# Spectral layer and gated FFN on one core: the stretch before the FFN's first product is rebuilt around two row pairs

## The chip, the cores and the metric

One core of a Trainium2 chip. The metric is the device time of one execution in microseconds (us): 515.73 us before, the median of three runs (515.6 to 515.79). The engines are PE (matrix products), DVE (vector), ACT (activation), POOL (GpSimd) and SP, which here only issues transfers. PSUM is where PE writes its results; DVE and ACT read them from there.

## The reference, cut to what matters

```python
x = A_x                                   # 1 x 2048 x 576, bf16
X = rfft2(layernorm(x)) * (w_r + 1j*w_i)  # over rows and columns
h = x + irfft2(X)                         # bf16
a = layernorm(h)
out = h + (gelu(a @ w_gate) * (a @ w_up)) @ w_down     # 576 -> 4608 -> 576
```

The Fourier transforms are computed as matrix products with sine and cosine tables.

## The kernel before, in words

**Layout.** The 2048 rows of x are 16 tiles `h` of 128 rows by 576 columns, kept in `h_sb`. Two neighbouring tiles are a pair `g = h // 2` (0 to 7).

**Stages.** (1) Layer norm and forward transform, to about 60 us. (2) Inverse transform. `i3` (L541, L542) makes the two spectra `EO0` and `EO1`. `inv_cols(x, g)` (L567) multiplies one pair of one spectrum by column tables: six products of 128 x 290 into one PSUM tile `cs_ps`, which ACT scales into a bf16 tile `cs` (L576; for x=1, g=0 half is done by DVE, L578 and L579). `add_rows(g)` (L652) multiplies the `cs` tiles of a pair, x = 0 and 1, by row tables `G16`: sixteen products of 64 rows by 288 columns, into two PSUM tiles `y_ps`, one for each tile of the pair. `add_h` (L663, DVE) adds each to `h_sb`. (3) The FFN's layer norm of each tile: mean and variance by DVE (`stats2`: L118 to L120) or by two ACT passes whose sums POOL finishes (`stats_act`: L125, then L129 to L131); POOL takes the power -0.5 (L135, L136); DVE normalises the row with each block of 64 columns written twice (`norm2`, L677); a DMA transposes it into `hl` (`flip`, L689), four tiles to one `hl` of 512 columns. (4) The FFN in four chunks of four tiles. A chunk has 36 blocks: 18 products of 64 x 512 with gate and up weights into a PSUM tile `gu` (L758), gelu by ACT (L766), product by DVE into `P_sb` (L767). Then four times 72 products with `w_down` into `acc` (L778).

**What orders the work.** The order on each engine is written by hand: each engine runs its instructions in the order of the program and waits where one needs another. All PSUM tiles of stages 2 to 4 (`eo_ps`, `cs_ps`, `y_ps`, `gu`, `acc`) share four buffers, called "two"; a new tile waits until an older one has been read. `g_sb`, the gelu's output, has three buffers. SP issues in its own order: weight transfers (`load_wd`, `load_gu`) and the transposes of `flip`.

**Ahead of the first `gu` product**, which needs the transposed tiles 0 to 3, the kernel computes all 16 `inv_cols`, the `add_rows` of pairs 0 to 4, and the statistics, rows and transposes of tiles 0 to 3. The dictionary `todo` places the rest behind given blocks of the FFN: `add_rows` of pairs 5, 6, 7, and `stats2`, `norm2` and `flip` of tiles 4 to 15.

Of the kernel before, what the change touches and what calls it, by code (L numbers as in the profile page):

```python
# [9 lines left out]
ACT = mybir.ActivationFunctionType  # L10
# [10 lines left out]
P = 128  # L21
S = 2048
H = 16
# [17 lines left out]
def kernel_body(  # L41
# [24 lines left out]
    def two(name):  # L66
        return psum.tile([P, 2, 512], FP32, name=name, tag="two", bufs=3)
# [54 lines left out]
    def ln_act(h):  # L122
        for i, fn in ((0, ACT.Identity), (1, ACT.Square)):
            junk = roll.tile([P, D], BF16, name="junk", tag="junk", bufs=2)
            A.activation(junk[:], h_sb[:, h, :], fn, accum_out=sums[:, h, i : i + 1])  # L125
# [432 lines left out]
            )  # L558

    cs = {}  # L560

    def inv_cols(x, g):

        ps = two("cs_ps")
        for e in range(2):
            for jt in range(NJT):
                T.matmul(  # L567
                    ps[:, e, 0:JP],
                    lhsT=EO[x][:, e, jt, 2 * g : 2 * g + 2].rearrange("p h e k l -> p (h e k l)"),
                    rhs=DT[:, jt, :, e, :] if jt < 2 else DI[:, :, e, :],  # L570
                    start=(jt == 0),
                    stop=(jt == NJT - 1),
                )
        t = eop.tile([P, 2, JP], BF16, name="cs", tag="cs", bufs=H)
        if x == 0 or g:
            A.activation(t[:], ps[:, :, 0:JP], ACT.Copy, scale=Y_SCALE)  # L576
        else:
            A.activation(t[:, 0, :], ps[:, 0, 0:JP], ACT.Copy, scale=Y_SCALE)  # L578
            V.tensor_scalar(t[:, 1, :], ps[:, 1, 0:JP], Y_SCALE, None, op0=ALU.mult)  # L579
        cs[x, g] = t  # L580


    n = len(order)
    for i in range(n + 1):
        last = i >= n
        if not last:
            f2(order[i])
        if i == 0:
            twiddles()
        if 1 <= i <= n:  # L590
            f3(order[i - 1], 0)
        if i >= 3 and not last:
            i3(order[i - 3], 0)
        if 1 <= i <= n:
            f3(order[i - 1], 1)
            if i == 1:
                sums_of(order[0])
            else:
                wmul(order[i - 2], i - 1, order[i - 1])
        if i >= 3 and not last:  # L600
            i3(order[i - 3], 1)
        if not last:
            f2(order[i] + 8)
        if i == 0:
            weights()
        if i >= 3:
            for jt in range(0 if last else 2, NJT):
                i3(order[i - 3], jt)
        if last:
            wmul(order[i - 1], i)  # L610
        if i == 1:
            late_tables()
            scr_pool.__exit__(None, None, None)
            eop = ctx.enter_context(tc.tile_pool(name="eop", bufs=1, side="right"))
            EO = [eop.tile([P, 2, NJT, H, 2, 4, 8], BF16, name=f"EO{x}") for x in range(2)]
    for g in range(3):
        inv_cols(0, g)
    for jt in range(NJT):
        i3(order[6], jt)
    inv_cols(0, 3)  # L620
    inv_cols(0, 4)
    for jt in range(NJT):
        i3(order[7], jt)

    spw.__exit__(None, None, None)
    spec.__exit__(None, None, None)
    fp = ctx.enter_context(tc.tile_pool(name="ffn", bufs=1))
    P_sb = fp.tile([P, NFT, 4 * P], BF16, name="P_sb")
    wd_b = fp.tile([P, NFT - NWA, D], BF16, name="wd_b")

    def load_wd(f0):
        nc.sync.dma_start(wd_b[:, f0 : f0 + NWA, :], wd_view[:, NWA + f0 : 2 * NWA + f0, :])

    load_wd(0)


    ln2 = {}

    def add_rows(g):


        ys = [two("y_ps") for _ in range(2)]
        for b in range(2):
            for x in range(2):
                if b == 0:
                    cv = cs[x, g][:].rearrange("p t (q a) -> p t q a", q=2)[:, :, :, 0 : JH - 1]
                else:
                    cv = cs[x, g][:, :, 1:J].rearrange("p t (q a) -> p t q a", q=2)[:, :, :, ::-1]
                for t in range(2):
                    for i in range(2):  # L650
                        rows = slice(64 * i, 64 * i + 64)
                        T.matmul(  # L652
                            ys[i][:, b, 0:DH],
                            lhsT=G16[rows, b * t, x, :],
                            rhs=cv[rows, t],
                            start=(x == t == 0),
                            stop=(x == t == 1),
                        )
        return ys

    def add_h(h, ys):
        hv = h_sb[:, h, :].rearrange("p (b a q) -> p b q a", b=2, q=2)
        V.tensor_tensor(hv, hv, ys[h % 2][:, :, 0:DH].rearrange("p b (q a) -> p b q a", q=2), ALU.add)  # L663

    def add_both(g):
        ys = add_rows(g)
# [23 lines left out]
            hl[h // 4 % 2][:, :, q : q + P], ln2[h][:].rearrange("p r b k -> p (r b k)"), transpose=True  # L690
        )

    def stats_act(h):
        ln_act(h)
        ln_fin(mv2, h)
        ln_rstd(rstd2, mv2, h, h + 1)

    inv_cols(1, 0)
    inv_cols(1, 1)
    inv_cols(0, 5)  # L700
    ys = add_rows(0)
    add_h(0, ys)
    add_h(1, ys)
    stats2(0)
    inv_cols(1, 2)
    ys = add_rows(1)
    stats_act(1)
    inv_cols(0, 6)
    add_h(2, ys)
    norm2(0)  # L710
    flip(0)
    add_h(3, ys)
    inv_cols(0, 7)
    stats2(2)
    norm2(1)
    flip(1)
    inv_cols(1, 3)
    stats_act(3)
    inv_cols(1, 4)
    norm2(2)  # L720
    flip(2)
    inv_cols(1, 5)
    norm2(3)
    flip(3)
    load_wd(NWA)
    inv_cols(1, 6)
    add_both(2)
    inv_cols(1, 7)
    add_both(3)
    add_both(4)  # L730

    todo = {}
    for h in range(4, H):
        b = 6 * (h // 2 - 2)
        if h >= 10 and h % 2 == 0:
            todo.setdefault(b, []).append((add_both, h // 2))
        todo.setdefault(b, []).append((stats2, h))
        b = h // 4 * NFT - NFT + 3 * (h % 4) + 2 + 6 * (h < 8)
        todo.setdefault(b, []).append((norm2, h))
        todo.setdefault(b + 1, []).append((flip, h))  # L740

    blk = 0
    groups = pre
    NG = NFT // FQ
    for tcnk in range(4):
        for gi in range(NG):
            fa = gi * FQ
            w = groups.pop(0)
            n = tcnk * NG + gi + 2
            if 3 <= n < 4 * NG:  # L750
                groups.append(load_gu(n))
            for i in range(FQ):

                gu = two("gu")
                for r in range(NR):
                    for c in range(2):
                        rows = slice(64 * c, 64 * c + 64)
                        T.matmul(  # L758
                            gu[:, c, :],
                            lhsT=w[rows, r, i * P : (i + 1) * P],  # L760
                            rhs=hl[tcnk % 2][rows, r, :],
                            start=(r == 0),
                            stop=(r == NR - 1),
                        )
                g_sb = roll.tile([P, 4 * P], FP32, name="g_sb", tag="g_sb", bufs=3)
                A.activation(g_sb[:], gu[:, 0, :], ACT.Gelu_apprx_tanh)  # L766
                V.tensor_tensor(P_sb[:, fa + i, :], g_sb[:], gu[:, 1, :], ALU.mult)  # L767
                for fn, h in todo.pop(blk, ()):
                    fn(h)
                blk += 1  # L770
        for st in range(4):
            h = tcnk * 4 + st
            last = h == H - 1
            acc = two("acc")
            for c in range(2):
                cc = slice(c * DH, (c + 1) * DH)
                for f in range(NFT):
                    T.matmul(  # L778
                        acc[:, c, 0:DH],
                        lhsT=P_sb[:, f, st * P : (st + 1) * P],  # L780
                        rhs=wd_a[:, f, cc] if f < NWA else wd_b[:, f - NWA, cc],
                        start=(f == 0),
                        stop=(f == NFT - 1),
                    )
                if last:
                    V.tensor_tensor(h_sb[:, h, cc], h_sb[:, h, cc], acc[:, c, 0:DH], ALU.add)  # L786
                    nc.sync.dma_start(out_view[:, h, cc], h_sb[:, h, cc])
            if not last:
                hv = h_sb[:, h, :].rearrange("p (b n) -> p b n", b=2)
                V.tensor_tensor(hv, hv, acc[:, :, 0:DH], ALU.add)  # L790
                if tcnk == 3:
                    nc.sync.dma_start(out_view[:, h, :], h_sb[:, h, :])
        if tcnk < 3:
            nc.sync.dma_start(
                out_view[:, tcnk * 4 : (tcnk + 1) * 4, :],
                h_sb[:, tcnk * 4 : (tcnk + 1) * 4, :],
            )
# [46 lines left out]
```

## Time and profile before

| | |
|---|---|
| runs | 515.6, 515.73, 515.79 us |
| profiled execution | 515.73 us; its span (first to last instruction) 514.0 us, so 1.7 us lie around it |
| busy share of the span | PE 97%, DVE 40%, ACT 30%, POOL 7% |
| granted PE clock | 0.999 of full speed |
| end of stage 1, start of the first `cs_ps` product | 60.6 us |
| first `gu` product | 84.67 us |
| one `gu` block on PE | 1.95 us (342 products in 37.08 us on the chain) |
| `add_rows` of a pair behind an FFN block | 0.99 us of PE (x16) |

Times in the trace are counted from the start of the span. Of each instruction, the profile has start, duration, what it waited for before it, and what waited for it. The chain of work is followed back from the last instruction to what released it; it gives the length of the stretches that set the end. Instructions of one engine overlap a little: the next one's record often starts before the former's ends, so the distance between two starts (the pitch) is shorter than a record.

### The profile page before, as it was taken

To read this page: it belongs to the slowest core of one execution; us is meant where nothing else is said; L and a number is where in the kernel's file an instruction comes from. 1 tells how busy PE (TensorE), PEld (TensorE's weight loads), DVE (VectorE), ACT (ScalarE), POOL (GpSimd) and SP (SyncE) were. 2 spreads that over 40 slices of the span, in tenths; PEclk is the share of its full clock that TensorE was granted. 3 is DMA by queue.
4 is the path that set the end of the run, shared out by engine and by line. 5 is a ranking of instruction groups with operands and counts; after the bars stand their busy time and mean duration, and the time that the engine had idled before them with its cause. 6 is when DMAs were issued, how large, how long until landed. Compare 5 with 4: busy or idle time off the path is not lost.

```text
span 514.0 us, 9918 instructions
## 1 busy us (share of the span) xinstructions
PE 498.3 (97%) x4369; PEld 295.3 (57%) x4369; DVE 206.5 (40%) x381; ACT 153.5 (30%) x262; POOL 34.6 (7%) x94
## 2 busy tenths in 40 slices
PE   6989998999999999999999999999999999999996
PEld 2457765555557774444467754444577544444774
DVE  8979957566551003533321034333301233333000
ACT  8688974322221002233310013323200132323000
POOL 8700012111110000000000000000000000000000
PEclk9999999999999999999999999999999999999999
DMA  8964049799772009998740069988600477780000
GB/s 282 244 132 138 1 140 229 141 186 186 142 143 61 1 1 190 191 200 157 159 76 0 1 148 182 210 155 157 120 1 0 110 156 161 157 156 2 13 13 24
DMA packets 88459, 61.25 MB, mean 119 GB/s; under 512 B 24288, under 2 KB 87136, under 8 KB 88416
## 3 DMA queue, kind: packets, MB, share of 16 engines
q1 hardware_dynamic: 88128, 59.44, 56.8%
q0 software_dynamic: 288, 1.18, 0.8%
q8 instruction: 34, 0.56, 0.5%
q14 instruction: 9, 0.07, 0.1%
HBM read 52.65 MB, written 2.36 MB: 107 GB/s over the span
## 4 chain that ended last, share of the span: by engine, by line
PE 91%; DVE 5%; ACT 1%; POOL 1%; DMA 1%; issue 1%; POOLq 0%; DVEq 0%; ACTq 0%
PE gu L758 55%; PE acc L778 28%; PE f2t L259 2%; PE pq_ps L442 1%; PE cs_ps L567 1%; PE eo_ps L542 1%; PE eo_ps L541 1%; PE y_ps L652 1%; PE f2t L247 1%; DMA Bt<-hrow 1%; PE gh_ps L457 1%; PE gh_ps L458 1%; PE f L268 1%; DVE st L119 0%; DVE h_sb L663 0%
## 5 line engine op out<-in xcount | busy, mean ns | idle before, releaser
L758 PE MATMUL gu<-Bt,wgu 64*128 64x512 bf16 x2592 | 280.9, 376 | 0.7 <-DMA Bt<-hrow 0.7
L758 PEld LDWEIGHTS <-wgu 64*128 64x128 bf16 x2592 | 131.0, 94 | 148.6 <-issue 1.6
L766 ACT ACTIVATE g_sb<-gu 128x512 f32<-128x512 f32 x144 | 86.0, 597 | 305.9 <-PE gu L758 305.9
L767 DVE TENSOR_TENSOR P_sb<-g_sb,gu 128x512 bf16<-128x512 f32 x144 | 98.7, 685 | 162.1 <-ACT g_sb L766 162.1
L778 PEld LDWEIGHTS <-P_sb 128*128 128x128 bf16 x1152 | 112.4, 98 | 30.6 <-issue 2.4
L778 PE MATMUL acc<-wd_b,P_sb 128*128 128x288 bf16 x768 | 99.3, 286 | 0.0
L790 DVE TENSOR_TENSOR h_sb<-h_sb,acc 128x576 bf16<-128x576 bf16 x15 | 11.3, 754 | 119.2 <-PE acc L778 119.2
L778 PE MATMUL acc<-wd_a,P_sb 128*128 128x288 bf16 x384 | 52.3, 286 | 0.5 <-DVE h_sb L786 0.5
L247 PE MATMUL f2t<-h_sb,ident 128*128 128x512 bf16 x41 | 12.3, 422 | 4.5 <-DMA h_sb<-in_A_x_dram 4.5
L677 DVE TENSOR_SCALAR hrow<-h_sb,mv,rstd 128x1152 bf16<-128x1152 bf16 x16 | 13.8, 865 | 1.9 <-POOL rstd L136 1.9
L136 POOL TENSOR_TENSOR rstd<-rstd,mhalf 128x1 f32<-128x1 f32 (+2 forms) x21 | 14.0, 666 | 1.8
L567 PE MATMUL cs_ps<-DT,EO 128*128 128x290 bf16 x64 | 12.5, 286 | 0.6 <-DVE h_sb L663 0.4
L663 DVE TENSOR_TENSOR h_sb<-h_sb,y_ps 128x576 bf16<-128x576 bf16 x16 | 11.7, 784 | 2.1 <-PE y_ps L652 2.1
L135 POOL TENSOR_SCALAR rstd<-mv 128x1 f32<-128x1 f32 (+2 forms) x21 | 4.8, 230 | 113.4 <-DVE mv L120 112.6
L442 PE MATMUL pq_ps<-DT,Bt 128*128 128x290 bf16 x64 | 12.4, 287 | 0.0
L541 PE MATMUL eo_ps<-TI,Zt 128*128 128x256 bf16 x48 | 11.5, 272 | 0.4 <-DVE Zt L516 0.4
L542 PE MATMUL eo_ps<-TI,Zt 128*128 128x256 bf16 x48 | 11.5, 273 | 0.1
L567 PEld LDWEIGHTS <-EO 128*128 128x128 bf16 x96 | 8.9, 96 | 4.5 <-issue 1.3
L247 PEld LDWEIGHTS <-ident 128*128 128x128 bf16 x45 | 4.7, 104 | 11.4 <-issue 5.0
L259 PE MATMUL f2t<-F,xn 128*128 128x256 bf16 x64 | 9.7, 274 | 1.6 <-DVE xn L139 1.6
L125 ACT ACTIVATE junk<-h_sb 128x576 bf16<-128x576 bf16 x16 | 10.7, 670 | 1.4 <-DMA h_sb<-in_A_x_dram 0.9
L652 PE MATMUL y_ps<-cs,G 64*128 64x288 bf16 x128 | 9.8, 283 | 1.1 <-DVE h_sb L663 0.9
(113 smaller groups left out, 246.2 us busy)
## 6 DMA issues: line engine op xcount, KB each, us to landing
wgu<-in_B_w_gate_dram SPq DMA_DIRECT2D x48, 432.0 KB, 5.2
wgu<-in_B_w_up_dram SPq DMA_DIRECT2D x48, 432.0 KB, 6.6
wd_b<-in_B_w_down_dram SPq DMA_DIRECT2D x2, 1728.0 KB, 8.8
h_sb<-in_A_x_dram SPq DMA_DIRECT2D x3, 576.0 KB, 6.3
wd_a<-in_B_w_down_dram SPq DMA_DIRECT2D x1, 1728.0 KB, 9.1
out_dram<-h_sb SPq DMA_DIRECT2D x3, 576.0 KB, 3.4
WR<-in_A_w_r_dram SPq DMA_DIRECT2D x1, 650.2 KB, 9.1
WI<-in_A_w_i_dram SPq DMA_DIRECT2D x1, 650.2 KB, 11.5
```

What stands on the lines that cost most here:

```text
L136: G.tensor_tensor(dst[:, sl], dst[:, sl], mhalf[:, sl], ALU.pow)
L247: T.matmul(dst, lhsT=ident[:], rhs=h_sb[:, 2, 0:512], start=True, stop=True)
L259: T.matmul(f2t[:, h % 2, t * 2 * P : (t + 1) * 2 * P], lhsT=x[:, d0 : d0 + P], rhs=F16[:, n : n + 2, :], start=(n == 0), stop=(n == 1),)
L442: T.matmul(ps[:, par, 0:JP], lhsT=Bt[:, t, col], rhs=DT[:, t // 2, par] if t < 4 else DF[:, par], start=(t == par), stop=(t == 4),)
L541: T.matmul(ps[:, b], lhsT=zl(*z0), rhs=TI[:, kk_, 1:3, :], start=True, stop=False)
L542: T.matmul(ps[:, b], lhsT=zl(*z1), rhs=TI[:, kk_, 0:2, :], start=False, stop=True)
L567: T.matmul(ps[:, e, 0:JP], lhsT=EO[x][:, e, jt, 2 * g : 2 * g + 2].rearrange("p h e k l -> p (h e k l)"), rhs=DT[:, jt, :, e, :] if jt < 2 ...
L652: T.matmul(ys[i][:, b, 0:DH], lhsT=G16[rows, b * t, x, :], rhs=cv[rows, t], start=(x == t == 0), stop=(x == t == 1),)
L758: T.matmul(gu[:, c, :], lhsT=w[rows, r, i * P : (i + 1) * P], rhs=hl[tcnk % 2][rows, r, :], start=(r == 0), stop=(r == NR - 1),)
L766: A.activation(g_sb[:], gu[:, 0, :], ACT.Gelu_apprx_tanh)
L767: V.tensor_tensor(P_sb[:, fa + i, :], g_sb[:], gu[:, 1, :], ALU.mult)
L778: T.matmul(acc[:, c, 0:DH], lhsT=P_sb[:, f, st * P : (st + 1) * P], rhs=wd_a[:, f, cc] if f < NWA else wd_b[:, f - NWA, cc], start=(f == 0 ...
```

## The change

- `inv_cols` writes its columns in another order (undoing the even and odd split of the column transform) and the pairs in two forms: pairs 0 and 1 as bf16 tiles `cs`, two to a product; pairs 2 to 7 as fp32 tiles `cw`, scaled by ACT in one instruction.
- Ahead of the FFN only `add_rows` of pairs 0 and 1 stay. For pairs 2 to 7 the new `fold` (DVE, four `tensor_tensor` of 128 x 288, fp32 in, bf16 out, for each pair) adds and subtracts the two halves first, so that `add_rows` needs eight products where it had sixteen. The folds go behind the FFN's blocks 2 to 7, the `add_rows` behind blocks 4, 10, 16, 22, 28, 34.
- For tiles 0 to 3 the addition `add_sum` is one DVE instruction that also sums the row, with one ACT pass for the sum of squares; `head_rstd` (two DVE instructions of 128 x 1, two on POOL) takes the place of `stats2` and `stats_act`.
- Tiles 0 and 1 are transposed by DMA as before. Tiles 2 and 3 are transposed by PE (`turn`: 18 products of 64 x 128 into a PSUM tile, copied to `hl` by ACT, 5 blocks of 128, and DVE, 4 blocks).
- The `inv_cols` stand in another order, and `w_down` lies in three tiles; the last third is loaded behind block 12, into the place of five `cw` tiles.

```diff
     def inv_cols(x, g):
...
-        t = eop.tile([P, 2, JP], BF16, name="cs", tag="cs", bufs=H)
-        if x == 0 or g:
-            A.activation(t[:], ps[:, :, 0:JP], ACT.Copy, scale=Y_SCALE)
-        else:
-            A.activation(t[:, 0, :], ps[:, 0, 0:JP], ACT.Copy, scale=Y_SCALE)
-            V.tensor_scalar(t[:, 1, :], ps[:, 1, 0:JP], Y_SCALE, None, op0=ALU.mult)
-        cs[x, g] = t
+        pv = ps[:, :, 0:JP].rearrange("p t (q a) -> p t q a", q=2)
+        if g >= 2:
+            if x == 0 or g == 2:
+                cw[x, g] = eop.tile([P, 2, JP], FP32, name=f"cw{x}{g}")[:]
+            else:
+                cw[x, g] = cwb[:, g - 3]
+            A.activation(
+                cw[x, g].rearrange("p t (a q) -> p t q a", q=2), pv, ACT.Copy, scale=Y_SCALE
+            )
+            return
+        ts = [eop.tile([P, JP], BF16, name=f"cs{x}{g}{t}") for t in range(2)]
+        for t in range(2):
+            dst = ts[t][:].rearrange("p (a q) -> p q a", q=2)
+            if x == 1 and t == 1:
+                V.tensor_scalar(dst, pv[:, t], Y_SCALE, None, op0=ALU.mult)
+            else:
+                A.activation(dst, pv[:, t], ACT.Copy, scale=Y_SCALE)
+        cs[x, g] = ts
...
     for g in range(3):
         inv_cols(0, g)
-    for jt in range(NJT):
-        i3(order[6], jt)
+    for k in order[6:]:
+        for jt in range(NJT):
+            i3(k, jt)
     inv_cols(0, 3)
-    inv_cols(0, 4)
-    for jt in range(NJT):
-        i3(order[7], jt)
...
+    def fold(g):
+        if g in (2, 5):
+            both[g] = eop.tile([P, 3, 2, 2, DH], BF16, name=f"both{g}", tag=f"EO{g // 3}")
+        for x in range(2):
+            f0, f1 = cw[x, g][:, 0], cw[x, g][:, 1]
+            b = both[g - (g - 2) % 3][:, (g - 2) % 3, x]
+            V.tensor_tensor(b[:, 0, :], f0[:, 0:DH], f1[:, 0:DH], ALU.add)
+            V.tensor_tensor(b[:, 1, :], f0[:, DH:0:-1], f1[:, DH:0:-1], ALU.subtract)
+            both[x, g] = b
...
         for b in range(2):
...
+            steps = [(x, t) for x in range(2) for t in range(2 if g < 2 else 1)]
+            for s, (x, t) in enumerate(steps):
+                for i in range(2):
+                    rows = slice(64 * i, 64 * i + 64)
+                    T.matmul(
+                        ys[i][:, b, 0:DH],
+                        lhsT=G16[rows, b * t, x, :],
+                        rhs=cs[x, g][t][rows, sl[b]] if g < 2 else both[x, g][rows, b, :],
+                        start=(s == 0),
+                        stop=(s == len(steps) - 1),
+                    )
...
+    def add_sum(h, ys):
+        hv = h_sb[:, h, :].rearrange("p (b n) -> p b n", b=2)
+        V.scalar_tensor_tensor(
+            hv, ys[h % 2][:, :, 0:DH], 1.0, hv, op0=ALU.mult, op1=ALU.add, accum_out=sums[:, h, 0:1]
+        )
+        junk = roll.tile([P, D], BF16, name="junk", tag="junk", bufs=2)
+        A.activation(junk[:], h_sb[:, h, :], ACT.Square, scale=float(D) ** 0.5, accum_out=sums[:, h, 1:2])
...
+    def turn(h):
+        pt = psum.tile([P, 2048], BF16, name="pt", tag="two", bufs=4)
+        for r in range(NR):
+            for p0 in (0, 64):
+                T.transpose(pt[p0 : p0 + 64, r * P : (r + 1) * P], ln2[h][:, r * 64 : (r + 1) * 64], ident[:])
+        q = h % 4 * P
+        pv = pt[:, 0 : NR * P].rearrange("p (r q) -> p r q", r=NR)
+        A.copy(hl[0][:, 0:5, q : q + P], pv[:, 0:5])
+        V.tensor_copy(hl[0][:, 5:NR, q : q + P], pv[:, 5:NR])
...
     inv_cols(1, 0)
     inv_cols(1, 1)
+    y0 = add_rows(0)
+    y1 = add_rows(1)
+    add_sum(0, y0)
+    add_sum(1, y0)
+    inv_cols(0, 4)
+    add_sum(2, y1)
+    head_rstd(0)
+    add_sum(3, y1)
+    head_rstd(1)
     inv_cols(0, 5)
-    ys = add_rows(0)
-    add_h(0, ys)
-    add_h(1, ys)
-    stats2(0)
-    inv_cols(1, 2)
-    ys = add_rows(1)
-    stats_act(1)
-    inv_cols(0, 6)
-    add_h(2, ys)
     norm2(0)
     flip(0)
-    add_h(3, ys)
-    inv_cols(0, 7)
-    stats2(2)
+    head_rstd(2)
+    inv_cols(0, 6)
     norm2(1)
     flip(1)
-    inv_cols(1, 3)
-    stats_act(3)
-    inv_cols(1, 4)
-    norm2(2)
-    flip(2)
-    inv_cols(1, 5)
-    norm2(3)
-    flip(3)
-    load_wd(NWA)
+    head_rstd(3)
+    inv_cols(0, 7)
+    inv_cols(1, 2)
+    norm_row(2)
+    norm_row(3)
+    for g in range(3, 6):
+        inv_cols(1, g)
+    turn(2)
+    turn(3)
     inv_cols(1, 6)
-    add_both(2)
     inv_cols(1, 7)
-    add_both(3)
-    add_both(4)
...
     for h in range(4, H):
         b = 6 * (h // 2 - 2)
-        if h >= 10 and h % 2 == 0:
-            todo.setdefault(b, []).append((add_both, h // 2))
-        todo.setdefault(b, []).append((stats2, h))
-        b = h // 4 * NFT - NFT + 3 * (h % 4) + 2 + 6 * (h < 8)
+        if h % 2 == 0:
+            todo.setdefault(h // 2, []).append((fold, h // 2))
+            todo.setdefault(b + 4, []).append((add_both, h // 2))
+        todo.setdefault(b + 5 + h % 2, []).append((stats2, h))
+        b = h // 4 * NFT - NFT + 3 * (h % 4) + 2 + 12 * (h < 8)
         todo.setdefault(b, []).append((norm2, h))
         todo.setdefault(b + 1, []).append((flip, h))
+
+    todo.setdefault(12, []).append((last_wd, 0))
```

More of the change, by code (lines that the diff above doesn't have):

```diff
@@ L560, in kernel_body @@
     cs = {}
+    cw = {}
     def inv_cols(x, g):
@@ L614, in kernel_body @@
             eop = ctx.enter_context(tc.tile_pool(name="eop", bufs=1, side="right"))
-            EO = [eop.tile([P, 2, NJT, H, 2, 4, 8], BF16, name=f"EO{x}") for x in range(2)]
+            EO = [eop.tile([P, 2, NJT, H, 2, 4, 8], BF16, name=f"EO{x}", tag=f"EO{x}") for x in range(2)]
     for g in range(3):
         inv_cols(0, g)
-    for jt in range(NJT):
-        i3(order[6], jt)
+    for k in order[6:]:
+        for jt in range(NJT):
+            i3(k, jt)
     inv_cols(0, 3)
-    inv_cols(0, 4)
-    for jt in range(NJT):
-        i3(order[7], jt)
     spw.__exit__(None, None, None)
@@ L628, in kernel_body, with load_wd, last_wd @@
     P_sb = fp.tile([P, NFT, 4 * P], BF16, name="P_sb")
[L629 to L634, printed above, removed]
-    ln2 = {}
+    cwb = fp.tile([P, 5, 2, JP], FP32, name="cwb", tag="wd2")[:]
+    wd = [wd_a, fp.tile([P, NWA, D], BF16, name="wd_b")]
+    def load_wd(i):
+        nc.sync.dma_start(wd[i][:], wd_view[:, i * NWA : (i + 1) * NWA, :])
+    def last_wd(h):
+        wd.append(fp.tile([P, NWA, D], BF16, name="wd_c", tag="wd2"))
+        load_wd(2)
@@ new lines, in kernel_body @@
+    load_wd(1)
+    ln2 = {}
+    both = {}
+    def fold(g):
[7 more added lines that the diff above has]
+            both[x, g] = b
@@ L639, in add_rows @@
     def add_rows(g):
         ys = [two("y_ps") for _ in range(2)]
+        sl = (slice(0, DH), slice(DH, 0, -1))
         for b in range(2):
[L644 to L658, printed above, removed]
+            steps = [(x, t) for x in range(2) for t in range(2 if g < 2 else 1)]
[9 more added lines that the diff above has]
+                    )
@@ L659, in add_rows @@
         return ys
     def add_h(h, ys):
-        hv = h_sb[:, h, :].rearrange("p (b a q) -> p b q a", b=2, q=2)
-        V.tensor_tensor(hv, hv, ys[h % 2][:, :, 0:DH].rearrange("p b (q a) -> p b q a", q=2), ALU.add)
+        hv = h_sb[:, h, :].rearrange("p (b n) -> p b n", b=2)
+        V.tensor_tensor(hv, hv, ys[h % 2][:, :, 0:DH], ALU.add)
     def add_both(g):
@@ L691, in flip @@
         )
[L693 to L696, printed above, removed]
+    def add_sum(h, ys):
+        hv = h_sb[:, h, :].rearrange("p (b n) -> p b n", b=2)
+        V.scalar_tensor_tensor(
[3 more added lines that the diff above has]
+        A.activation(junk[:], h_sb[:, h, :], ACT.Square, scale=float(D) ** 0.5, accum_out=sums[:, h, 1:2])
@@ new lines, in head_rstd @@
+    def head_rstd(h):
+        V.scalar_tensor_tensor(
+            mv2[:, h, 1:2], sums[:, h, 0:1], sums[:, h, 0:1], sums[:, h, 1:2], op0=ALU.mult, op1=ALU.subtract
+        )
+        V.tensor_scalar(mv2[:, h, 0:1], sums[:, h, 0:1], 1.0 / D, None, op0=ALU.mult)
+        G.tensor_scalar(rstd2[:, h : h + 1], mv2[:, h, 1:2], -1.0 / (D * D), 1e-5, op0=ALU.mult, op1=ALU.add)
+        G.tensor_tensor(rstd2[:, h : h + 1], rstd2[:, h : h + 1], mhalf[:, h : h + 1], ALU.pow)
+    def turn(h):
[7 more added lines that the diff above has]
+        V.tensor_copy(hl[0][:, 5:NR, q : q + P], pv[:, 5:NR])
@@ L698, in kernel_body, with norm_row @@
+    def norm_row(h):
+        hrow = ln2[h] = roll.tile([P, D], BF16, name="hflat", tag="hrow", bufs=4)
+        normalise(V, hrow[:], mv2, rstd2, h)
     inv_cols(1, 0)
     inv_cols(1, 1)
-    inv_cols(0, 5)
-    ys = add_rows(0)
-    add_h(0, ys)
-    add_h(1, ys)
-    stats2(0)
-    inv_cols(1, 2)
-    ys = add_rows(1)
-    stats_act(1)
-    inv_cols(0, 6)
-    add_h(2, ys)
+    y0 = add_rows(0)
[4 more added lines that the diff above has]
+    add_sum(2, y1)
@@ L780, in kernel_body @@
                         lhsT=P_sb[:, f, st * P : (st + 1) * P],
-                        rhs=wd_a[:, f, cc] if f < NWA else wd_b[:, f - NWA, cc],
+                        rhs=wd[f // NWA][:, f % NWA, cc],
                         start=(f == 0),
```

## The prediction

> **What bounds the kernel now.** I read the clock first: 0.999 of full speed, 1.00 in every stretch I asked for, so products have one price. Then busy time by stretch; columns are length, then busy time and instructions of PE, PEld, DVE, ACT, POOL, then granted clock, DMA share, GB/s.
>
> ```profile
> 60.56:84.67 24.11, 21.77 (x203) 15.48 (x201) 16.01 (x33) 17.53 (x31) 4.38 (x14) 1.00 0.53 126
> 84.67:157.76 73.09, 73.09 (x697) 39.36 (x698) 42.55 (x83) 20.90 (x35) 9.37 (x24) 1.00 0.86 174
> 157.76:514.00 356.24, 351.81 (x3096) 206.68 (x3096) 93.42 (x134) 65.09 (x109) 0.00 (x0) 1.00 0.51 99
> ```
>
> From 84.67 on PE never waits: the kernel ends later or earlier by as much as the first `gu` product does, plus whatever PE work or waiting the change puts behind it. The stretch before holds 24.11 us, of which matmul records (with pipeline tails) cover 21.77. The chain there (start, length):
>
> ```profile
> 70.03 1.15 PE y_ps L652 x16
> 71.17 1.47 DVE h_sb L663 x2
> ...
> 75.04 0.87 DVE hrow L677
> 75.91 0.70 DVE h_sb L663
> ...
> 79.65 0.58 POOL rstd L136
> 80.25 0.87 DVE hrow L677
> 81.15 3.38 DMA Bt<-hrow
> 84.54 0.14 issue
> 84.67 5.34 PE gu L758 x47
> ```
>
> So the end of the head is tile 3: pair 1's product, two sums, statistics with POOL, the row, a transpose of 3.38 us. PE fills that time with `inv_cols` and row products, and waits only 0.7 us for the transpose. Shortening the chain alone gains little; PE's own work ahead of `gu` must go too. The change does both.
>
> **The price rows.**
>
> ```profile
> 78.05 1.72 ACT L576 ACTIVATE cs<-cs_ps 128x580 bf16<-128x580 f32 x3
> 35.37 0.30 PE L400 MATMUL pt<-ident,F 128*64 128x128 bf16 x4
> 87.46 0.69 DVE L767 TENSOR_TENSOR P_sb<-g_sb,gu 128x512 bf16<-128x512 f32 x1 [1.67 <-ACT g_sb L766]
> 88.06 0.45 DVE L118 BATCH_NORM_STATS2 st<-h_sb 128x6 f32<-128x288 bf16 x1
> 88.43 0.44 DVE L119 BATCH_NORM_STATS2 st<-h_sb 128x6 f32<-128x288 bf16 x1
> 5.79 1.07 DVE L219 TENSOR_TENSOR pd<-iD,iJ 128x870 f32<-128x870 f32 x1
> ```
>
> ACT evicts 580 columns in 0.65, at a pitch of 0.56 where work is queued. Starts on DVE stand 0.60 apart behind an L767 of 0.69, and 0.37 behind an L118 of 0.45: the overlap is 0.08 to 0.09. An `inv_cols` is six products at 0.124, 0.745; a pair's sixteen row products are 0.98 (0.061 each).
>
> **Part 1, order up to the row products.** Until 64.11 PE does what it did. Then come the 12 products of `i3` for k=0 (0.11 each, the third and fourth held by DVE's second half of `Zt` at 64.32 and 64.56): 65.6. Three `inv_cols`, (0,3), (1,0), (1,1), 2.24: 67.8. Their covers: (0,3) needs the tile ACT frees at 65.5; (1,0)'s third product needs the last `EO` eviction, ACT at 66.5, when PE gets there at 66.57. Before, (1,0) stalled twice (0.39 and 0.17), and (0,4) and (0,5) stood ahead. Row products start at 67.9, where they started at 69.96: **2.05 earlier**. Pairs 0 and 1 take 1.96: 69.9. The evictions they need (68.2 and 68.9, from the 0.41 and 0.46 of L578 and L579) come as PE arrives.
>
> **Part 2, sums and statistics.** From the first row product to the first sum took 1.20 before; so `add_sum` starts at 69.1. No row shows its accumulator on DVE. Bounds: 0.71 (L663's pitch, sum free) and 1.1 (0.78, 0.19 as ACT's accumulator read, no overlap). I take 0.88, ACT's case (0.67 and 0.19 at a pitch of 0.69) being the nearest. The sums end at 70.0, 70.9, 71.7 and, behind two 128 x 1 instructions (0.15 each in L213 to L217), 73.0. ACT's pass over tile 3 then runs 73.05 to 73.75, and queued behind it stand the evictions of (0,5), (0,6), (0,7), (1,2): 73.75, 74.3, 74.9, 75.4. PE runs (0,4) to (0,7) and (1,2) from 70.1 to about 74.0, must wait at (1,3) for the tile that the first of these frees (74.40), and ends (1,5) at 76.7: 0.7 lost. DVE in the meantime writes row 0 by 74.1, row 1 by 75.3, rows 2 and 3 by 76.0 and 76.8 (0.87 and 0.48 each, POOL's 0.9 beside other work).
>
> **Part 3, transposes on PE.** 36 products of 64 x 128. L400 has the very shape: four start within 0.1, 0.026 each; a pair of L268 takes 0.18 with the switch, 0.09 each. I take 0.045, nearer L400 since they run in a row: 1.6, and 0.15 for the switch: 78.45. (1,6) and (1,7) cover the copies to `hl` (ACT 0.7, DVE 0.6 each) and end at 80.05. DMA transposes of tiles 0 and 1 issue at 74.1 and 75.3 and land 3.4 later, 78.7: hidden by 1.4. The gelu table (1.28) ends as the first block does. **First `gu` at 80.15, 4.5 earlier.**
>
> **Part 4, behind the start of the FFN.** On PE six times eight row products, 2.93, replace three times 0.99: nothing. On DVE 24 fold instructions land in blocks 2 to 7. L219 is the nearest row, fp32 both ways: 1.07 for 870 is 0.906 at one column a cycle (0.96 in a ns, as L767's 512 in 0.53 plus its fixed part) and 0.164 fixed; 288 columns give 0.464, at a pitch of 0.375. Bounds: 0.30 (the columns alone) and 0.46 (L579, 290 columns, no overlap).
> DVE's queue from block 2's L767, which starts 6.70 after the first `gu` product (three blocks of 1.95, 0.21, 0.60, 0.03), to that of block 9: eight L767 at 0.60 and 0.09, two sums at 0.71, two `stats2` at 0.95, 24 folds at 0.375 make 17.2, and with 0.1 for the signal 24.0. A block needs 1.95 on PE and 2.1 on DVE with a fold, up to 3.5 with sums: DVE falls behind. PE would want to start block 11 at 22.47 (eleven blocks, two pairs of row products). With four PSUM tiles, pair 3's second row tile waits for block 8's L767 and block 11 for block 9's. So PE stands **1.5 us** there, once; from block 8 on DVE gains 1.3 a block and catches up. Blocks 3 to 10 wait for nothing late: block 10 needs block 6's L767 at 18.1 and starts at 20.0. SP: the last third of `w_down` (8.8 to landing) issues near 104 and is needed at about 150; weights for a block group are asked for 11.7 ahead (6.6 to landing). The tail is untouched.
>
> [...]
>
> **Sum.** -4.5 + 1.5 = -3.0 from 515.73 (profiled execution and median are the same): **512.7 us**.
>
> **Rivals.**
> - *Folds do not overlap* (0.46): stall 1.5 + 24 x 0.085 = 3.5; 514.8. For: L579. Against: every queued DVE pair overlaps. 0.13.
> - *Slower: ACT's new store order.* `cs` and `cw` are written to every second column; no row writes so. If that halved ACT's rate (580 columns 1.13, pitch 1.04), evictions would set PE's pace from (0,3) on: row products at 70.1, sums done at 74.8, evictions from 75.9 at 1.04, (1,7) at 84.1, the last copy to `hl` 84.5, the table at 87.9, 1.1 after block 0. 84.6 - 84.67 + 1.5 + 1.1 = +2.5: 518.2. It turns into a loss when an eviction takes above about 0.9. Against: L450 reads in another order (0.66) and L550 writes runs of eight (0.59 for 512) at the full rate. 0.11.
> - *The chain stays with the DMA.* FFN transposes took 6.4 in the middle, up to 8.9, beside weight loads. With 8.9 row 1 lands at 84.2, the gain is 0.4 and the stall stays: 516.8. Against: `w_down`'s second third, issued at 65.6, lands by 74.4, before both. 0.07.
> - *The clock falls.* If the transposes left the clock at half, the 3.3 us from them to `gu` would double: 516.0. Against: 1.00 even in 81.0 to 84.6, where PE ran 2.15 of 3.60. 0.05. [...]
>
> My forecast has 0.64. The range takes in folds at 0.46 with sums at 1.1 (515.7) and, below, transposes at 0.026 (0.7), sums at 0.71 (0.7) and half the stall (510.6): **510.6 to 516.0**. Within 0.2% (1.03 us, about what a measurement can tell) is 514.7 to 516.8: faster 0.74, same 0.12, slower 0.14.
>
> **What would show it.** Row products at 67.9 (part 1); a pitch of four `add_sum` near 0.88 and (1,3) waiting for ACT (part 2); 36 transposes in 1.6 and `gu` at 80.15 with no DMA wait (part 3); one PE wait of about 1.5 at block 10 or 11, for DVE's L767 (part 4). I am wrong if ACT's evictions exceed 0.9, or if PE waits in blocks 3 to 9.

## The result, and the profile after

| | before | after |
|---|---|---|
| median of the runs | 515.69 us (515.6 to 515.79) | 512.53 us (512.41 to 512.78) |
| profiled execution, its span | 515.73, 514.0 us | 512.41, 510.4 us |
| first `cs_ps` product of the head | 60.67 us | 60.50 us |
| first `gu` product | 84.67 us | 78.88 us |
| first `acc` product | 157.69 us | 154.27 us |

The ratio is 0.9939 (0.9922 to 0.9957): 3.2 us faster, where 3.0 were forecast (512.7). The table has the starts of the records; the chain counts a product that follows another up to 0.2 us later (78.95, 157.76 and 154.34), and the stretches below are cut there. Runs of one kernel fall on two levels some 1.5 us apart (before, in a later set of 17: 515.5 to 515.9 at a mean granted clock of 0.998 to 1.000, and 516.8 to 517.3 at 0.996), so that a difference under about 0.5 us between two experiments is not read, and a median can lie between the levels.

The same three stretches as in the prediction, of the kernel after: length, busy time and instructions of PE, PEld, DVE, ACT, POOL, then granted clock, DMA share, GB/s.

```profile
60.50:78.95 18.45, 18.45 (x192) 13.92 (x191) 12.16 (x36) 16.57 (x33) 3.11 (x8) 1.00 0.48 129
78.95:154.34 75.39, 73.92 (x697) 36.43 (x698) 51.90 (x105) 22.91 (x38) 8.13 (x20) 1.00 0.92 169
154.34:510.40 356.06, 351.81 (x3096) 206.68 (x3096) 95.53 (x141) 65.09 (x109) 1.56 (x4) 1.00 0.52 99
```

Line 1: the head is 5.7 us shorter, and PE has no gap left in it; before, 2.3 of its 24.1 us had no matmul record. Line 2: the first chunk of the FFN is 2.30 us longer (73.09 before) and PE is idle in it for 1.5 us by record, where it had no gap at all. With the rest 0.18 shorter (behind the last sum, where the output is stored: 3.7 us to the end of the span, 3.8 before): -5.72 + 2.30 - 0.18 = -3.6 of span, -3.3 in the profiled times. So 40% of what the head gained is given back behind it. The chain shows the head, and where the FFN loses:

```profile
70.10 6.12 PE cs_ps L568 x48
76.22 1.13 PE pt L745 x36
77.35 1.60 PE cs_ps L568 x12
78.95 5.95 PE gu L814 x54
...
101.25 0.61 DVE P_sb L823
101.90 0.65 PE y_ps L678 x7
...
124.89 10.26 DMA wgu<-in_B_w_up_dram
135.19 2.13 PE gu L814 x17
```

From 60.67 to 84.9 the chain is PE alone. Then it runs through DVE's queue up to 101.9, where a row product of pair 3 waits for the product of block 8. Later it leaves PE for up-projection weights that took 10 us to land, at 135 and in the same way at 148. The view of waits gives both (total, times, longest):

```profile
PE y_ps L678 <- DVE P_sb L823: 0.9, 1, 0.9
...
PE gu L814 <- DMA wgu<-in_B_w_up_dram: 0.6, 2, 0.3
```

These are idle times after the modelled end of the last product. From start to start the cost is a little more: 1.09 at pair 3 (eight products stand 0.06 apart, here 100.75 and 101.90), and about 0.5 at each weight.

Why the weights are late is in SP's (SyncE's) queue (start, length of the issue; the last two lines are of the kernel before):

```profile
106.02 0.57 SPq L644 DMA_DIRECT2D wd_c<-in_B_w_down_dram  x1
110.47 0.60 SPq L147 DMA_DIRECT2D wgu<-in_B_w_gate_dram  x1
111.12 0.74 SPq L147 DMA_DIRECT2D wgu<-in_B_w_up_dram  x1
112.61 6.71 SPq L715 DMA_TRANSPOSE Bt<-hrow  x1
```

```profile
82.51 0.58 SPq L632 DMA_DIRECT2D wd_b<-in_B_w_down_dram  x1
...
110.32 1.94 SPq L689 DMA_TRANSPOSE Bt<-hrow  x1
```

The last third of `w_down` (1728 KB, 13.0 us to landing) is issued behind block 12. The transpose behind it holds the queue for 6.71 us (1.3 to 2.0 in the kernel before, whose last third went out at 82.51), and the next weight load goes out behind it, at 119.43.

### The profile page after: what moved, and what is told of

The parts are those of the page before. It is cut to its first block, busy times and chain, and to the rows that moved or that the text cites. A ratio compares the mean times of both kernels' runs of the same rounds, so it can differ in the third digit from the quotient of the medians.

```text
span 510.4 us, 9927 instructions
## 1 busy us (share of the span) xinstructions
PE 496.5 (97%) x4357; PEld 291.1 (57%) x4357; DVE 214.1 (42%) x414; ACT 154.6 (30%) x266; POOL 33.2 (6%) x88
## 3 DMA queue, kind: packets, MB, share of 16 engines
q0 software_dynamic: 288, 1.18, 0.8%
## 4 chain that ended last, share of the span: by engine, by line
PE 87%; DVE 7%; DMA 4%; ACT 1%; issue 0%; SPq 0%; POOL 0%; POOLq 0%; ACTq 0%; DVEq 0%
PE gu L814 48%; PE acc L834 28%; DMA wgu<-in_B_w_up_dram 4%; PE cs_ps L568 2%; PE f2t L259 2%; PE pq_ps L442 1%; PE eo_ps L542 1%; PE eo_ps L541 1%; DVE both L665 1%; DVE both L664 1%; DVE P_sb L823 1%; PE y_ps L678 1%; PE f2t L247 1%; PE gh_ps L457 1%; PE gh_ps L458 1%; PE f L268 1%
## 5 line engine op out<-in xcount | busy, mean ns | idle before, releaser
L814 PEld LDWEIGHTS <-wgu 64*128 64x128 bf16 x2592 | 128.4, 94 | 151.5 <-DMA wgu<-in_B_w_up_dram 1.6
L834 PE MATMUL acc<-wd_b,P_sb 128*128 128x288 bf16 x384 | 52.3, 286 | 0.0
L834 PE MATMUL acc<-wd_c,P_sb 128*128 128x288 bf16 x384 | 52.3, 286 | 0.0
L247 PE MATMUL f2t<-h_sb,ident 128*128 128x512 bf16 x41 | 12.9, 441 | 4.4 <-DMA h_sb<-in_A_x_dram 4.4
L703 DVE TENSOR_SCALAR hrow<-h_sb,mv,rstd 128x1152 bf16<-128x1152 bf16 x14 | 12.1, 866 | 0.5 <-POOL rstd L737 0.5
L136 POOL TENSOR_TENSOR rstd<-rstd,mhalf 128x1 f32<-128x1 f32 (+2 forms) x17 | 11.9, 697 | 1.4
L247 PEld LDWEIGHTS <-ident 128*128 128x128 bf16 x45 | 4.9, 108 | 11.7 <-issue 5.6
L442 PEld LDWEIGHTS <-Bt 128*128 128x128 bf16 x96 | 9.2, 97 | 2.5
L450 ACT CAST pq<-pq_ps 128x580 bf16<-128x580 f32 x15 | 9.9, 660 | 0.9 <-PE pq_ps L442 0.8
```

The costliest lines, as they stand in the source:

```text
L136: G.tensor_tensor(dst[:, sl], dst[:, sl], mhalf[:, sl], ALU.pow)
L247: T.matmul(dst, lhsT=ident[:], rhs=h_sb[:, 2, 0:512], start=True, stop=True)
L442: T.matmul(ps[:, par, 0:JP], lhsT=Bt[:, t, col], rhs=DT[:, t // 2, par] if t < 4 else DF[:, par], start=(t == par), stop=(t == 4),)
L703: V.tensor_scalar(hrow[:], h_sb[:, h, :].rearrange("p (r k) -> p r k", k=64).unsqueeze(2).to_broadcast([P, NR, 2, 64]), mv2[:, h, 0:1], rs ...
L814: T.matmul(gu[:, c, :], lhsT=w[rows, r, i * P : (i + 1) * P], rhs=hl[tcnk % 2][rows, r, :], start=(r == 0), stop=(r == NR - 1),)
L834: T.matmul(acc[:, c, 0:DH], lhsT=P_sb[:, f, st * P : (st + 1) * P], rhs=wd[f // NWA][:, f % NWA, cc], start=(f == 0), stop=(f == NFT - 1),)
```

## The experiments

The theory after the result: the head gained by PE work moved out, by a shorter chain of statistics and by two tiles turned on PE; the FFN lost 1.1 us to DVE, behind bunched folds, and 1.0 us to `w_down`'s last third among the weight loads. The rivals: the losses belong to something else (DMA transposes that now stand six blocks later, sums), or the gains of the parts are not what they were taken for. All times are medians, to be set against 512.53 of the changed kernel.

### Folds further apart

```diff
-            todo.setdefault(h // 2, []).append((fold, h // 2))
+            todo.setdefault(2 * (h // 2) - 3, []).append((fold, h // 2))
```

> The folds of pairs 2 to 7 go behind FFN blocks 1, 3, 5, 7, 9 and 11 instead of 2 to 7; nothing else moves. Theory: the bunched folds put VectorE behind, so that TensorE waited 1.09 us at 101.0 to 101.9 in the changed kernel (pair 3's second row tile behind the product of block 8). With a block of about 2.1 us between two folds of some 1.5 us of VectorE time each that backlog does not build up: the wait goes and the time falls by 1.1 us, to about 511.4. The two waits for up-projection weights at 135 and 148 us (1.0 us together) stay. Rival: the wait is not made by the bunching but by the eviction and adds of pair 3 itself; then it stays and the time is the same within 0.3 us.

Measured: 511.21 us, 1.3 less. The first chunk takes 74.1 instead of 75.4, and the wait for DVE is gone. DVE now waits for ACT between folds, which shows that it has no backlog (kernel with folds apart, DVE's timeline):

```profile
87.69 0.69 DVE L823 TENSOR_TENSOR P_sb<-g_sb,gu 128x512 bf16<-128x512 f32 x1 [1.12 <-ACT g_sb L822]
```

The weight waits stay (0.6 in the view of waits, as in the changed kernel). The theory holds.

### The last third of w_down later

```diff
-    todo.setdefault(12, []).append((last_wd, 0))
+    todo.setdefault(25, []).append((last_wd, 0))
```

> The load of the last third of w_down is issued behind FFN block 25 (about 131 us) instead of block 12 (106.0 us); its first use is at 157.2 us. Theory: that transfer, issued in front of the transposes of tiles 4 to 7 and the next weight tiles on SyncE's queue, holds them up (the first transpose behind it took SyncE's queue 6.71 us), and so the weights for the blocks at 135 and 148 us come 0.5 us late each; moved, both waits go and the time falls by 1.0 us, to about 511.5, while VectorE's 1.09 us stay. Rival: the waits come from the transposes, which now stand 6 blocks later than before; then they stay, and the time is the same within 0.3 us. Second rival: the transfer collides with the weights wherever it is put; then a wait of about the same size appears between 135 and 155 us.

Measured: 514.25 us, where the theory said 1.0 less than 512.53. This median lies between three runs of 513.45 to 513.65, at a mean clock of 1.0, and three of 514.85 to 515.17, at 0.995 or 0.996: 1.1 more where the clock held, 2.6 where it fell. The second rival had the place right and the size wrong: one wait, longer than the two it replaces. The kernel with the late load, PE's timeline and then its stretches:

```profile
149.35 5.74 PE L814 MATMUL gu<-Bt,wgu 64*128 64x512 bf16 x35 [1.90 <-DMA wgu<-in_B_w_up_dram]
```

```profile
150.00:151.00 1.00, 1.00 (x8) 0.41 (x6) 0.00 (x0) 0.00 (x0) 0.00 (x0) 0.57 1.12 184
151.00:152.00 1.00, 1.00 (x6) 0.31 (x4) 0.00 (x0) 0.00 (x0) 0.00 (x0) 0.50 1.16 206
```

The DMA engines are busy there (share above 1.1). No transpose stands behind the load here, and still the up-projection weights issued right behind it took 12.9 us to land: sharing the DMA engines is enough to make them late. And the 35 products behind the wait take 5.74 us instead of 4.05: in this run the clock was granted at half for 3.4 us. Putting off the load was the wrong direction: it meets the weight loads there too.

### The transposes of tiles 4 to 7 back where they were

```diff
-        b = h // 4 * NFT - NFT + 3 * (h % 4) + 2 + 12 * (h < 8)
+        b = h // 4 * NFT - NFT + 3 * (h % 4) + 2 + 6 * (h < 8)
```

> The normalisation and DMA transposes of tiles 4 to 7 go back to where the kernel before has them, behind blocks 8, 11, 14 and 17 (instead of 14, 17, 20, 23); the last third of w_down stays behind block 12. Theory (the w_down transfer is what delays the weights): one transpose still stands behind the transfer and pays several us of SyncE's queue; the weight waits stay between 0.4 and 1.0 us, and the normalisations, now ahead of or among the folds' late adds, can add a VectorE wait of up to 1 us: 512.0 to 513.5. Rival (the place of the transposes makes the waits): both waits go and the time falls by about 1.0 us, to 511.5.

Measured: 514.24 us, above both expectations. The weight waits did not go, they grew to 1.5 us (longest 1.0), and a wait of 0.7 for DVE came on top, because a normalisation (0.87) now stands right behind block 8, where DVE is still late. The place of the transposes alone is not the cause, and the rival falls. The theory's range was too low: it allowed for the wait for DVE, but not for weight waits beyond 1.0.

### Both edits

> Both edits of the first two kernels together: folds behind blocks 1, 3, 5, 7, 9, 11 and the last third of w_down behind block 25. Theory: the two losses are independent, VectorE's 1.09 us and the weights' 1.0 us, so both go: 512.53 - 2.1 = about 510.4. Rival: taking away one loss only uncovers the other (weights that arrive late leave VectorE time to catch up, or an earlier TensorE meets the same weights later); then only the larger of the two single gains is left, 511.4.

Measured: 513.08 us, 1.2 less than the late load alone, as the folds apart bring on their own. The two losses are independent, but the expected 510.4 failed with late_w_down's: the second edit is no cure.

### The last third of w_down earlier

```diff
-    P_sb = fp.tile([P, NFT, 4 * P], BF16, name="P_sb")
-    cwb = fp.tile([P, 5, 2, JP], FP32, name="cwb", tag="wd2")[:]
+    P_ab = fp.tile([P, 2 * NWA, 4 * P], BF16, name="P_ab")
+    cwb = fp.tile([P, 5, 2, JP], FP32, name="cwb", tag="pc")[:]
...
-    todo.setdefault(12, []).append((last_wd, 0))
+    todo.setdefault(1, []).append((last_wd, 0))
+    todo.setdefault(2 * NWA - 1, []).append((new_pc, 0))
```

(`wd_c` has a tile of its own; `new_pc` makes the last third of the product tile in `cwb`'s place.)

> The last third of w_down gets a tile of its own and is issued behind FFN block 1 (about 82 us) instead of block 12; the fp32 tiles that the folds read lie in the last third of the product tile P_sb instead (a tile of its own, first written behind block 23). Folds, transposes and all else stay. Why: late_w_down showed that the transfer collides with the weight loads later too, so its place is not wrong by being too early. Theory: from 105 us on the weight loads alone nearly fill the DMA engines (share 1.1 to 1.2 from 110 to 150 us), and 1.7 MB more there make the weights late; from 79 to 90 us the share is 0.34, and put there the transfer costs nothing: both waits go, -1.0 us, to 511.5. Rival: the weights are late by themselves (loads asked for too late); then both waits stay and the time is 512.5.

Measured: 510.98 us, 1.55 less, 0.5 beyond the expected. No weight wait is left. The load was issued at 76.6, right behind the two transposes (its tile is its own now, so that it waits for nothing), and landed in 9.5 us. The stretch that the load entered and the one that it left, first of the changed kernel, then of this one:

```profile
79.00:90.00 11.00, 11.00 (x108) 5.11 (x106) 5.83 (x13) 4.94 (x7) 0.00 (x0) 1.00 0.34 70
...
110.00:120.00 10.00, 10.00 (x99) 5.43 (x96) 6.71 (x12) 2.98 (x5) 0.04 (x1) 1.00 1.10 273
```

```profile
79.00:90.00 11.00, 11.00 (x107) 5.17 (x108) 5.66 (x13) 5.07 (x8) 0.00 (x0) 1.00 0.78 218
...
110.00:120.00 10.00, 10.00 (x98) 5.48 (x96) 6.57 (x13) 2.98 (x5) 0.01 (x1) 1.00 0.84 159
```

The DMA share falls from 1.10 to 0.84 from 110 to 120 us and rises from 0.34 to 0.78 from 79 to 90, where nothing waits for it. A high share alone does not make weights late: from 120 to 140 it is still 1.18 and 1.10 in this kernel, and PE waits for none. What is gone is the load in front of the transposes, which now land in 5.9 us instead of 9.2 (median of the five from 76 us on). The first chunk takes 74.3, 1.1 less, which is the theory's 1.0. The rest lies behind the last sum, in the store of the output: 3.2 us to the end of the span instead of 3.7. It is 3.3 in late_w_down, early_flips and no_folds too, and 3.7 in spread_folds; what sets it is not shown.

### Both cures

> early_w_down with the folds behind blocks 1, 3, 5, 7, 9 and 11 as well. Theory: both losses of the changed kernel go, 511.21 (spread_folds) - 1.0 = 510.2. Rival: the weights stay late, 511.2.

Measured: **509.72 us** (509.54 to 509.79), ratio to the kernel before 0.9874 (0.9853 to 0.9896). The first chunk is 73.0 us, as before the change (73.0), and PE waits for nothing between 60 and 157 us. This is the best version: the change's head without what it gave back, 2.8 us under the changed kernel.

### Tiles 2 and 3 turned by DMA again

```diff
-    norm_row(2)
-    norm_row(3)
+    norm2(2)
+    flip(2)
+    norm2(3)
+    flip(3)
...
-    turn(2)
-    turn(3)
```

> Tiles 2 and 3 are normalised and transposed through the DMA queue, as tiles 0 and 1 are, instead of on TensorE. Theory: the statistics of tile 3 are there near 76.2 us, its transpose stands behind three others of 1.4 us each on SyncE's queue and lands near 81; the first FFN product starts at about 81.2 instead of 78.9, so the time rises by 2.3 us (1.5 to 3.5), to 514.8. Rival: the DMA transposes are hidden behind the last row products, and the 36 transposes' 1.13 us on TensorE are saved: 511.4.

Measured: 515.65 us, 3.1 more: nothing is left of the gain against before. PE's timeline of this kernel:

```profile
81.65 8.59 PE L814 MATMUL gu<-Bt,wgu 64*128 64x512 bf16 x52 [3.75 <-DMA Bt<-hrow]
```

The first `gu` product starts at 81.65, 2.8 later (expected 2.3). In this profile, of a run of 517.2, the clock was also halved from 80.5 to 87.4: 52 products take 8.59 us.

To see what the halved clock is worth, the gap was filled with products that nobody reads:

```diff
+    fill = two("fill")
+    for _ in range(28):
+        T.matmul(fill[:, 0, 0:DH], lhsT=ident[:], rhs=cs[0, 0][0][:, 0:DH], start=True, stop=True)
```

> dma_turn with 28 more products of 128 x 288 on TensorE between the last of the inverse column sums and the first FFN product, into a tile that nobody reads: they fill most of the 3.7 us in which TensorE waited there for the transposes. They add work and take no wait away. Theory: in dma_turn the granted clock fell to 0.50 from 80.6 to 87.7 us because TensorE had nothing to do from 77.9 to 81.6; filled, the clock stays at 1.00, and the time falls by what the halved clock costs, to about 513.8 (from 515.65). Rival: the clock falls for another reason, or the filling only delays the first FFN product; then the time is 515.5 or more.

Measured: 515.56 us, the same. The profile of the filled kernel, of a run of 515.09, has the clock at 1.00 throughout and still starts late:

```profile
77.41 3.59 PE L786 MATMUL fill<-cs,ident 128*128 128x288 bf16 x28
81.24 9.03 PE L817 MATMUL gu<-Bt,wgu 64*128 64x512 bf16 x82 [0.24 <-DMA Bt<-hrow]
```

The filling is not what delays `gu`: it ends first, and `gu` still waits 0.24 for the transposes. The theory that most of the loss beyond 513.8 is the clock falls. The mean clock is below 0.998 in eleven of the twelve runs of dma_turn and in three of the twelve here, and the medians are the same. What costs is that the transposes land late: 2.4 us of `gu`'s start here, and 2.6 of span (513.0). That the clock's fall adds so little fits the weights: in dma_turn's profile PE, held up by the clock, waits for none of them, here 0.9 us for two. This balance is argued from two profiles, not shown. One run of each kernel took 513.84 and 513.98 with the clock at 1.00; why these two were so much shorter stays open.

### The former statistics

```diff
-    add_sum(0, y0)
-    add_sum(1, y0)
+    add_h(0, y0)
+    add_h(1, y0)
+    stats2(0)
+    stats_act(1)
```

(tiles 2 and 3 likewise, and no `head_rstd`)

> Row sums of tiles 0 to 3 by the former way: the adds without accumulated sums, then the two-pass statistics on VectorE (tiles 0 and 2) and ScalarE (1 and 3); transposes of tiles 2 and 3 stay on TensorE. Theory: in the changed kernel TensorE never waits for the statistics by the record, with 32 row products and 12 sums left as cover, and what the accumulated sums save is mostly hidden; but tile 3's chain has only some 1.1 us to spare, and the former statistics take 1.5 to 2.5 us more: +1.0 us (0 to 2.0), to 513.5. Rival: all hidden, within 0.3 us.

Measured: 513.55 us, 1.0 more, as expected; from the first `cs_ps` to the first `gu` 19.4 instead of 18.4. But the place is another one than I named. PE waits 0.39 for DVE's sums and 0.37 for an eviction that stands behind ACT's passes:

```profile
76.39 0.41 PE L568 MATMUL cs_ps<-DT,EO 128*128 128x290 bf16 x2 [0.37 <-ACT cw L581]
...
78.72 1.20 PE L745 MATMUL pt<-ident,hflat 128*64 128x128 bf16 x36
```

The 36 transposes then start right behind (1,5) and do not wait for tile 3. So in this trace the accumulated sums help by leaving DVE and ACT to the evictions, not by bringing tile 3's row early.

### The order of the column sums

```diff
-    for k in order[6:]:
-        for jt in range(NJT):
-            i3(k, jt)
+    for jt in range(NJT):
+        i3(order[6], jt)
     inv_cols(0, 3)
+    for jt in range(NJT):
+        i3(order[7], jt)
```

> The inverse column sums of pair 3's first half stand between the products of the last two row tiles of the third stage again, as in the kernel before, instead of behind both; the rest is the changed kernel. Theory: the short waits behind the evictions of these products come back, about 0.5 us: 513.0. Rival: the order only shifts who waits, within 0.3 us of 512.53.

Measured: 513.08 us, 0.55 more, as expected. With the head's start equal (60.7) the row products start at 68.5 instead of 68.0 in spread_folds; (1,0) waits for the last `EO` eviction again:

```profile
66.61 0.55 PE L568 MATMUL cs_ps<-DT,EO 128*128 128x290 bf16 x2 [0.16 <-ACT EO L555]
```

### No folds

```diff
-            if x == 0 or g == 2:
-                cw[x, g] = eop.tile([P, 2, JP], FP32, name=f"cw{x}{g}")[:]
-            else:
-                cw[x, g] = cwb[:, g - 3]
+            cw[x, g] = eop.tile([P, 2, JP], BF16, name=f"cw{x}{g}")[:]
...
-            steps = [(x, t) for x in range(2) for t in range(2 if g < 2 else 1)]
+            steps = [(x, t) for x in range(2) for t in range(2)]
...
-            todo.setdefault(h // 2, []).append((fold, h // 2))
```

> The changed kernel without folds: pairs 2 to 7 are stored in bf16 and go through sixteen row products each instead of eight behind the folds. Theory: six pairs times 0.49 us of TensorE are added (2.9 us), VectorE's wait of 1.1 us goes, and of the two weight waits (1.0 us) about half, since TensorE asks later: 512.53 + 2.9 - 1.1 - 0.5 = 513.8. Rival: row products are hidden behind something else, so that folding only costs; then 511.4.

Measured: 512.81 us, only 0.3 more (expected 1.3). A pair's sixteen row products cost PE what was forecast, but both weight waits are gone, not half of them: counted from the first `gu` product, PE comes to these two blocks about 0.7 us later (four and five pairs at 0.49, less DVE's wait), and each wait was 0.5. The first chunk is 76.0 instead of 75.4, and the store at the end 0.4 shorter.

> early_w_down without folds. Nothing waits for weights there, so only two terms are left: + 2.9 for the row products, - 1.1 for VectorE's wait: 510.98 + 1.8 = 512.8. Rival: VectorE's wait is not made by the folds and stays: 513.9.

Measured: 512.80 us, 1.8 more than early_w_down, to the tenth as expected. With folds apart instead, 3.1 less (509.72). So the folds are worth 3 us of PE, of which the changed kernel kept 0.3: of the 2.8 that it lost, 2.1 went to the two waits that they, and the place they took from `w_down`, brought, and 0.4 lies in the store at the end; what makes up the rest is under what two medians tell apart here.

## Why the prediction was right, point by point

It was right in the sum (512.7 against 512.53) and in most of its mechanisms; four terms of it were mis-sized: two made the head 1.3 too long, one the stall 0.4 too long, and one left out 1.0 for the weights. That these cancel to 0.2 is luck.

- **Part 1, row products 2.05 earlier (67.9):** 67.77, of which 0.16 is an earlier start of the head. Right; the order alone is worth 0.55.
- **Part 2, `add_sum` at a pitch of 0.88, (1,3) waiting 0.7 for ACT:** the pitch was 0.68, below the lower bound of 0.71, so the last sum was done at 72.0 instead of 73.0, ACT's passes were out of the evictions' way, and the 0.7 did not come. The step that failed is the choice of ACT's accumulator read (0.19) as the nearest row:

```profile
69.03 0.76 DVE L723 SCALAR_TENSOR_TENSOR h_sb<-y_ps,h_sb 128x576 bf16<-128x576 f32 x1
69.71 0.08 DVE L723 DVE_READ_ACCUMULATOR h_sb<-y_ps,h_sb 128x1 f32 x1
69.71 0.76 DVE L723 SCALAR_TENSOR_TENSOR h_sb<-y_ps,h_sb 128x576 bf16<-128x576 f32 x1
```

  DVE's read takes 0.08 and the next sum starts beside it.
- **Part 3, transposes 1.6 and 0.15, `gu` at 80.15:** 36 took 1.13 (0.031 each; L400's 0.026 was nearer than the 0.045 I took), and `gu` came at 78.88. The head beat the forecast by 1.27: 0.62 here, 0.55 because the transposes start at 76.15 instead of 76.7, and 0.1 in what stands behind them. The 0.15 for the switch was an estimate; in the trace the first transpose starts 0.21 behind the last product (76.15, 75.94), where products follow at 0.124, so 0.09. That the DMA transposes of tiles 0 and 1 are hidden was right; dma_turn shows that those of tiles 2 and 3 would not have been.
- **Part 4, folds at a pitch of 0.375, one PE stall of 1.5 at block 10 or 11:** a record of 0.45 and a pitch of 0.37; one stall at pair 3's second row tile, for block 8's product, 1.09. Mechanism and place right, size 0.4 too large. Of the forecast's price for a record (0.464), the trace of before bears out the 0.96 columns in a ns: 288 columns more cost 0.299 us (means of 0.754 at 576, L790, and 0.455 at 288, L786). That this is one column a cycle no run shows. spread_folds shows that the bunching makes it.

```profile
86.16 0.45 DVE L664 TENSOR_TENSOR both<-cw 128x288 bf16<-128x288 f32 x1
86.52 0.45 DVE L665 TENSOR_TENSOR both<-cw 128x288 bf16<-128x288 f32 x1
```

- **Part 4, SP: weights "asked for 11.7 ahead (6.6 to landing)", `w_down` costed at nothing:** this step failed: a term put at nothing that cost 1.0. I compared each transfer with its own due time and with landing times of a queue that did not hold the other. Issued together, `w_down` took 13.0 instead of 8.8, the late weights 10, the transposes held the queue for 2.6 to 6.7, and two blocks lost 0.5 each. I had priced its moving past SP's queue only for itself. early_w_down shows it.
- **Rivals:** *folds do not overlap* is out (0.37 against 0.46). *ACT's store order*, with fp32 in place of bf16 for pairs 2 to 7, costs 0.03 to 0.12 an eviction (0.68 to 0.77 for 580 columns, 0.65 before), far from double. *The clock falls* with the transposes is out: 1.00 from 76 to 77 us, where most of them run. What a longer run of transposes does to the clock is not shown by so short a stretch: plain waits of 1.0 to 1.3 us left it alone too. The record of one transpose of 64 x 128 is 0.22 us, and they follow each other at 0.031.

The sum again: forecast -4.5 + 1.5 = -3.0; by the trace -5.72 + 1.09 + 1.0, with 0.2 more in the first chunk and 0.2 less behind it, -3.6 of span and -3.3 of the profiled time.

## What to carry to other kernels

When a load gives up its early place because its buffer is needed, price it with everything that shares its queue and its DMA engines at the new place, not against its own due time: here 1.7 MB moved from a stretch whose DMA share is 0.34 without it, into one of 0.84 with weights and transposes behind it in the queue, cost 1 us, and moving it still later cost 1.1 more (2.6 where the clock fell). Work that is taken off PE and given to another engine counts only if that engine is not bunched up when PE needs it next; spreading the same folds over twice as many blocks brought 1.3 us. And a head is shortened by taking away PE work and the chain together: each part of the head taken back alone cost 0.5 to 3.1 us.

## What the runs showed of the hardware

- **A short wait can halve PE's clock.** In all fourteen profiles PE waits 1.6 us at 28 us for ACT. In two of them (no_folds and old_statistics) the clock is at half behind it (0.50 and 0.52 of full speed from 30 to 32 us), in the others not (1.00). The stretch from 30 to 32 us of no_folds, and the same of the kernel after:

```profile
30.00:32.00 2.00, 2.00 (x7) 0.87 (x6) 0.49 (x1) 0.95 (x1) 0.00 (x0) 0.50 0.08 23
```

```profile
30.00:32.00 2.00, 2.00 (x16) 1.35 (x14) 0.49 (x1) 1.25 (x2) 0.00 (x0) 1.00 0.09 18
```

  Seven products and sixteen in the same time. After waits of 1.9 us (late_w_down, spread_and_late) it fell in both profiles, for 3.4 us, and by the mean clock in three of the six runs of each kernel; in the wait of 3.75 us (dma_turn) for 6.8. After waits of 1.0 to 1.3 us it never fell in a profile, nor after 1.6 and 1.7 us at 14 us (before, no_folds_early_w_down). One such drop costs 1.7 us (5.74 instead of 4.05 for the same 35 products). What decides whether a wait of 1.6 or 1.9 us is enough, no run shows.
- **A DMA transpose issued behind a large load holds its queue:** the first one behind the 1.7 MB took 6.71 us in the changed kernel, 5.99 in spread_folds and 6.67 in early_flips, against 1.32 to 1.99 for those of tiles 4 to 7 in the kernel before and 1.55 to 2.23 in late_w_down, though weight loads are under way there too.
- **An accumulated sum is nearly free on DVE:** a read of 0.08 us, beside the next instruction, and a pitch of 0.68 (0.71 for the plain addition before).
